# Order and queues of the first loads in an attention and two-MLP kernel

## Chip, cores and metric

The kernel runs on one core of a Trainium2 chip. The metric is the device time of one execution in microseconds; several runs are taken and their median counts.

## What is computed

Causal attention with a bias from running sums, for 4 batches of 8 heads, 576 positions and 64 channels, then two MLPs over the 2304 tokens of 512 channels (2048 inside): the first gated by a clipped linear function, the second by x times its sigmoid.

```python
def _attn_ref(q, k, v, s):
    scores = scale * np.matmul(q, k.transpose(0, 1, 3, 2))
    cum = np.cumsum(np.maximum(s, 0.0), axis=-1)
    bias = -(cum[:, :, :, None] - cum[:, :, None, :])
    scores = np.where(causal, -1000000000.0, scores + np.minimum(bias, 0.0))
    attn = softmax(scores)
    return np.matmul(attn, v)

def _moe_ref(x, w_in, w_out):
    h = x @ w_in
    return (h * np.clip(h + 3.0, 0.0, 6.0) / 6.0) @ w_out

def _moe2_ref(x, w_in, w_out):
    h = x @ w_in
    return (h / (1.0 + np.exp(-h))) @ w_out
```

The weights come in as 64-bit floats. A raw chunk of them (128 x 512 numbers, 512 KB) is turned into 32-bit floats on the chip and split into a high and a low part for the matmuls.

## The kernel before

**Stages.** The queries of a batch are cut into a part A (positions 0 to 255) and a part B (256 to 511, with the last 64 as a tail). A `Head` is one head of one batch and part, and there are 64 of them; the eight of part A of batch 0 come first. The plan runs in slots: nine slots with a head alone, then slots with a head and a step of the first MLP (`first` and `second`, lines 245 to 301). In a slot the current head's scores, mask, maximum and exps are made, the head before it is transposed and multiplied by its v (`av`), and the one before that is put in its place.

**Heads.** `Head.load` (line 394) issues q, k and, for the first 14 heads, v into one tile with a place of its own (lines 413, 414 and 403, 64 KB each). `load_cum` (line 416) puts two rows of running sums below q and k (line 423), which the score matmul (line 512) reads together with them. The first four heads take these rows from the tile `pairs` on the chip, later ones from its copy in memory, `pair_d` (stored at line 875). `pairs` is made from s: load (341), clip and scale (342), scan into `crow` (345), and two copies of it, one on VectorE (349) and one on ScalarE (350). In slot k the head k + 2 is loaded.

**Raw chunks.** `Feed.tick` (line 199) moves the chunks through a pipeline: `load` (147), `fields` on ScalarE and POOL (159 to 161), `join` on VectorE (172 and 176), and two ticks later `high` on ScalarE (120) and `low` on VectorE (187). Three ticks are made before the first slot, then 0.4 in a slot for nine slots, then two. The MLP steps of block 0 use two chunks each.

**Queues and order.** All of these transfers are issued by SP. The program gives the instructions in an order that serves as a priority; a scheduler places them on the engines, and an instruction whose inputs its own model takes to be ready can pass an earlier one. Each engine then runs its list in order. `keep_clock` (line 83) issues matmuls on constants; 34 of them stand at the start, and slots without an MLP step have three each.

Of the kernel before, what the change touches and what calls it, by code (L numbers as in the profile page):

```python
# [11 lines left out]
I32 = mybir.dt.int32  # L12
# [10 lines left out]
def f32(ap):  # L23
    return ap.bitcast(F32)
# [3 lines left out]
def kernel(  # L28
# [15 lines left out]
    nc = tc.nc  # L44
# [10 lines left out]
    T1 = 256  # L55
# [23 lines left out]
    busy = gpool.tile([P, 1024], BF16, tag="gl", name="busy")  # L79
# [3 lines left out]
    def keep_clock(n, beside):  # L83
        for _ in range(n):
            o = idle[:, : beside.shape[-1]]
            nc.tensor.matmul(o, busy[:, :P], beside, start=True, stop=True)
# [1 line left out]
    def heads_of(x):  # L88
        return x.bitcast(BF16).rearrange("p (n two) -> p n two", two=2)[:, :, 1]

    keep_clock(34, busy[:, :512])

    NZ = (NFULL - 1) * P
    cmask = cpool.tile([P, NZ + P], F32, tag="cmask", name="cmask")
# [18 lines left out]
    def pool_copy(o, i):  # L113
        nc.gpsimd.tensor_scalar(  # L114
            out=o, in0=i, scalar1=1.0, scalar2=1.0, op0=ALU.mult, op1=ALU.mult
        )
# [13 lines left out]
    class Chunk:  # L130
        def __init__(self, kind, m, f):
            self.key = (kind, m, f)
            self.src = ((w1i, w1o), (w2i, w2o))[m][kind == "o"][f]
            self.nm = f"{kind}{m}_{f}"
            self.home = wpool, f"{kind}{f}"
# [2 lines left out]
            pool, tag = self.home  # L138
            return pool.tile(shape, dt, tag=tag, name=f"{name}{self.nm}")

        def load(self):
            if self.src.dtype == F32:
                self.val = self.place([P, DM], F32, "raw")
                nc.sync.dma_start(self.val, self.src)
            else:
                raw = self.place([P, 2 * DM], I32, "raw")
                nc.sync.dma_start(raw, self.src.bitcast(I32))
                words = raw.rearrange("p (n two) -> p n two", two=2)
                self.words = words[:, :, 0], words[:, :, 1]

# [38 lines left out]
    class Feed:  # L189


        def __init__(self, keys, hi_eng, lo_eng):
            self.ch = [Chunk(*k) for k in keys]
            self.hi_eng, self.lo_eng = hi_eng, lo_eng
            self.t = 0

        def done(self):
            return self.t >= len(self.ch) + 3 + 2

        def tick(self):  # L200
            n = len(self.ch)
            t = self.t - 3
            lo = self.lo_eng[t % len(self.lo_eng)] if 0 <= t - 2 < n else ""
            if lo:
                self.ch[t - 2].high(self.hi_eng[t % len(self.hi_eng)])
            if 0 <= t < n:
                self.ch[t].fields()
            if lo == "p":
                self.ch[t - 2].low(lo)
            if 0 <= t - 1 < n:  # L210
                self.ch[t - 1].join()
            if lo == "v":
                self.ch[t - 2].low(lo)
            if self.t < n:
                self.ch[self.t].load()
            self.t += 1


# [112 lines left out]
    def bank(kind, shape, name):  # L331
# [6 lines left out]
    srow, crow = [  # L338
        wpool.tile([BH, S], F32, tag=f"{kd}{NF // 2 - 1}", name=f"{kd}row") for kd in "io"
    ]  # L340
# [5 lines left out]
    pairs = wpool.tile([BH, 2, 2 * T1], F32, tag=f"o{NF // 2 - 2}", name="pairs")  # L346
    nc.gpsimd.memset(pairs[:, 0, :T1], 1.0)
    nc.gpsimd.memset(pairs[:, 1, T1:], -1.0)
    nc.vector.tensor_copy(pairs[:, 0, T1:], crow[:, :T1])
    nc.scalar.copy(pairs[:, 1, :T1], crow[:, :T1])  # L350

    def split_rows():

# [16 lines left out]
    class Head:  # L370
# [20 lines left out]
                    (c, 0, w // 2, False), (c, w // 2, w, True)]  # L391
            self.full = [c for c in self.chunks if c < NFULL]

        def load(self):
            b, h, nm, nk, nq = self.b, self.h, self.nm, self.nk, self.nq
            if self.at < 14:

                t = wpool.tile([P, 2 * DM], F32, tag=spare[self.at], name=f"in{nm}")
                self.q2, self.k2 = t[:, :nq], t[:, nq : nq + nk]
                self.qk = t[:, : nq + nk]  # L400
                self.va = t[:, DM + nk :][:, : self.nkc * D].rearrange("p (c d) -> p c d", d=D)
                self.load_qk()
                nc.sync.dma_start(self.va, v1[b, h, :, : self.nkc, :])
                return
            tags = ("qs", "kl") if self.whole and self.slot else ("q2", "k2")
            self.q2 = apool.tile([P, nq], F32, tag=tags[0], name=f"q2{nm}")
            self.k2 = apool.tile([P, nk], F32, tag=tags[1], name=f"k2{nm}")
            self.load_qk()

        def load_qk(self):  # L410
            b, h, nk = self.b, self.h, self.nk
            for r in (slice(0, D), slice(D, 2 * D))[: 1 if self.whole else 2]:
                nc.sync.dma_start(self.q2[r, :], qT[b, h, :, self.q0 : nk])
                nc.sync.dma_start(self.k2[r, :], kT[b, h, :, :nk])

        def load_cum(self):

# [356 lines left out]
    heads = []  # L774
# [3 lines left out]
    feed = Feed([(kd, 0, f) for f in range(NF) for kd in "io"], "a", "v")  # L778
# [3 lines left out]
    def ticks(n):  # L782
        for _ in range(n):
            if not feed.done():
                feed.tick()
# [79 lines left out]
    def at(i):  # L865
        return heads[i] if 0 <= i < len(heads) else None


    loaded = 2
    for hd in heads[:loaded]:  # L870
        hd.load()
    ticks(3)
    for hd in heads[:loaded]:
        hd.load_cum()
    nc.sync.dma_start(pair_d, pairs)
    heads[0].places()
    k = 0
    p1 = p2 = None
    plan = [(True, False)] * (H + 1) + [(i < 55, True) for i in range(68)]
    nslot = 0  # L880
    for has_head, has_step in plan:
        cur = at(k) if has_head else None
        nx = at(k + 1) if has_head else None
        loads = []
        while has_head and loaded < len(heads) and loaded <= k + (
            2
        ):
            loads.append(heads[loaded])
            loaded += 1
        k += has_head and cur is not None  # L890
        tk = [0, 0, 0, 0]
        if not feed.done():
            rate = ((0.4,)*9+(2,))[min(nslot, len(((0.4,)*9+(2,))) - 1)]
            for i in range(4):
                feed_at += rate / 4
                tk[i] = int(feed_at)
                feed_at -= tk[i]
        slot(cur, p1, p2, nx, loads, has_step, tk)
        if nslot == 9:
            split_rows()  # L900
        p1, p2 = cur, p1
        nslot += 1
        if nslot == H + 1:
            p2.av_sum()
            p2 = None
            split1(0)
            turns["s"] = turns["s"][:1]
        if has_step and step in first_step[1:NB1]:
            blk = first_step.index(step)
            assert k - (cur is not None) >= (blk + 1) * H  # L910
            if p2:
                p2.av_sum()
                p2 = None
            if blk == NB1 - 1:
                cx.close()
                xpool = cx.enter_context(
                    tc.tile_pool(name="xlast", bufs=1, side="right", reuse_waits="tile")
                )
            split1(blk)
            if blk == NB1 - 1:  # L920
                break
# [70 lines left out]
    feed = Feed([("o", 1, f) for f in range(NF)], "a", "v")  # L992
# [293 lines left out]
```

## Time and profile before

| | us |
|---|---|
| median of 3 runs | 999.63 |
| lowest and highest | 997.51 and 1001.86 |
| the profiled execution | 1000.54 |
| span of the profiled execution | 998.8 |
| TensorE busy (matmuls) | 970.8 |
| VectorE busy | 737.9 |
| ScalarE busy | 511.0 |
| POOL busy | 317.2 |

The profile is of one execution. PE is TensorE's matmuls, PEld its weight loads, DVE VectorE, ACT ScalarE, POOL GpSimd; SPq and ACTq are the queues on which SP and ScalarE issue DMAs. Times in the trace count from the start of the span. A wait is put down to the releaser that came last by the profile; where a transfer is named that the instruction does not read, it was another one beside it.

### The profile page before, as it was taken

To read this page: it belongs to the slowest core of one execution; us is meant where nothing else is said; L and a number is where in the kernel's file an instruction comes from. 1 tells how busy PE (TensorE), PEld (TensorE's weight loads), DVE (VectorE), ACT (ScalarE), POOL (GpSimd) and SP (SyncE) were. 2 spreads that over 40 slices of the span, in tenths; PEclk is the share of its full clock that TensorE was granted. 3 is DMA by queue.
4 is the path that set the end of the run, shared out by engine and by line. 5 is a ranking of instruction groups with operands and counts; after the bars stand their busy time and mean duration, and the time that the engine had idled before them with its cause. 6 is when DMAs were issued, how large, how long until landed. Compare 5 with 4: busy or idle time off the path is not lost.

```text
span 998.8 us, 17929 instructions
## 1 busy us (share of the span) xinstructions
PE 970.8 (97%) x6268; PEld 891.6 (89%) x6268; DVE 737.9 (74%) x1757; ACT 511.0 (51%) x1177; POOL 317.2 (32%) x323
## 2 busy tenths in 40 slices
PE   8899989999999999999999999999999999999997
PEld 5789979999999999999997877899988989889996
DVE  6899998888789888988866799887574434743343
ACT  6898554555455555555446656564443323432332
POOL 4457853443333443434425566532000000000000
PEclk9999999999999999999999999999999999999999
DMA  5796112312222223222215957434354233442421
GB/s 174 225 302 198 47 40 67 92 46 63 83 77 75 71 59 92 60 64 80 60 39 186 392 212 237 163 116 190 133 195 169 77 145 110 167 154 76 148 74 64
DMA packets 54419, 125.41 MB, mean 126 GB/s; under 512 B 12332, under 2 KB 34076, under 8 KB 51000
## 3 DMA queue, kind: packets, MB, share of 16 engines
q1 hardware_dynamic: 53880, 123.60, 37.3%
q8 instruction: 50, 0.82, 0.3%
q10 hardware_dynamic: 448, 0.66, 0.2%
q14 instruction: 41, 0.34, 0.1%
HBM read 99.52 MB, written 24.69 MB: 124 GB/s over the span
## 4 chain that ended last, share of the span: by engine, by line
PE 70%; DVE 11%; DMA 8%; issue 4%; POOL 4%; SPq 3%; ACT 1%; POOLq 0%; DVEq 0%; ACTq 0%
PE a L1083 6%; PE a L1084 6%; PE a L1085 6%; PE h L1066 5%; PE h L1068 5%; PE h L1067 5%; PE ph L260 4%; PE ph L261 4%; PE ph L262 4%; PE acc L299 4%; PE acc L300 4%; PE acc L301 4%; PE poB L672 4%; DMA rawi<-in_w1i_dram 3%; POOL rawo L161 2%
## 5 line engine op out<-in xcount | busy, mean ns | idle before, releaser
L260 PE MATMUL ph<-xh,wi 128*128 128x256 f32 (+1 forms) x512 | 154.1, 303 | 3.2 <-DVE g L273 3.1
L300 PE MATMUL acc<-gl,wo 128*128 128x256 f32 (+1 forms) x512 | 151.1, 297 | 2.4 <-DVE gl L280 2.4
L261 PE MATMUL ph<-xl,wi 128*128 128x256 f32 (+1 forms) x512 | 151.6, 296 | 0.0
L262 PE MATMUL ph<-xh,wi 128*128 128x256 f32 (+1 forms) x512 | 151.3, 296 | 0.0
L301 PE MATMUL acc<-gh,wo 128*128 128x256 f32 (+1 forms) x512 | 149.8, 294 | 0.0
L1125 ACT ACTIVATE gh<-h 128x384 fp32r<-128x384 f32 x96 | 50.3, 524 | 185.4 <-DVE h L1133 185.3
L299 PE MATMUL acc<-gh,wo 128*128 128x256 f32 (+1 forms) x512 | 143.8, 297 | 0.0
L1083 PE MATMUL a<-wo,gh 128*128 128x512 f32 x288 | 113.5, 394 | 1.4 <-ACT gh L1125 0.9
L1084 PE MATMUL a<-wo,gh 128*128 128x512 f32 x288 | 113.1, 393 | 0.0
L260 PEld LDWEIGHTS ph<-xh,wi 128*128 128x128 f32 x512 | 97.4, 190 | 8.9 <-DVE g L273 2.5
L300 PEld LDWEIGHTS acc<-gl,wo 128*128 128x128 f32 x512 | 96.4, 188 | 6.4 <-DVE gl L280 3.5
L262 PEld LDWEIGHTS ph<-xh,wi 128*128 128x128 f32 x512 | 97.6, 191 | 3.0
L261 PEld LDWEIGHTS ph<-xl,wi 128*128 128x128 f32 x512 | 97.5, 190 | 3.2
L301 PEld LDWEIGHTS acc<-gh,wo 128*128 128x128 f32 x512 | 96.5, 189 | 3.3
L299 PEld LDWEIGHTS acc<-gh,wo 128*128 128x128 f32 x512 | 95.6, 189 | 3.4
L161 POOL TENSOR_SCALAR rawi<-rawi 128x512 int32<-128x512 f32 x32 | 70.0, 2188 | 74.1 <-ACT magi L160 48.4
L1085 PE MATMUL a<-wo,gl 128*128 128x512 f32 x288 | 90.0, 392 | 0.0
L161 POOL TENSOR_SCALAR rawo<-rawo 128x512 int32<-128x512 f32 x32 | 74.5, 2329 | 48.0 <-ACT mago L160 46.3
L1127 DVE TENSOR_TENSOR gl<-h,gh 128x384 fp32r<-128x384 f32 x96 | 53.8, 560 | 39.9 <-ACT h L1126 38.2
L114 POOL TENSOR_SCALAR gh<-g 128x512 fp32r<-128x512 f32 x68 | 50.6, 745 | 92.6 <-DVE g L273 77.4
L1133 DVE TENSOR_TENSOR h<-h,u 128x384 f32<-128x384 f32 x72 | 40.1, 557 | 53.5 <-PE h L1068 53.2
L1066 PE MATMUL h<-x0t,w 128*128 128x384 f32 x192 | 64.9, 338 | 0.7 <-DVE u L1133 0.7
(220 smaller groups left out, 2554.6 us busy)
## 6 DMA issues: line engine op xcount, KB each, us to landing
w<-w_d SPq DMA_DIRECT2D x18, 1792.0 KB
w_d<-w SPq DMA_DIRECT2D x8, 1792.0 KB
k2B<-in_kT_dram SPq DMA_DIRECT2D x64, 144.0 KB
rawi<-in_w1i_dram SPq DMA_DIRECT2D x16, 512.0 KB
rawo<-in_w1o_dram SPq DMA_DIRECT2D x16, 512.0 KB
rawi<-in_w2i_dram SPq DMA_DIRECT2D x16, 512.0 KB
rawo<-in_w2o_dram SPq DMA_DIRECT2D x16, 512.0 KB
q2B<-in_qT_dram SPq DMA_DIRECT2D x64, 80.0 KB
```

Source lines behind the costliest of these rows:

```text
L161: nc.gpsimd.tensor_scalar(out=high, in0=f32(high), scalar1=0.0, scalar2=float(SIGN), op0=ALU.is_lt, op1=ALU.mult,)
L260: nc.tensor.matmul(o, wih[:, cs], xh[c], start=c == 0, stop=False)
L261: nc.tensor.matmul(o, wih[:, cs], xl[c], start=False, stop=False)
L262: nc.tensor.matmul(o, wil[:, cs], xh[c], start=False, stop=c == NDC - 1)
L299: nc.tensor.matmul(a, woh[:, cs], gh[:, jj, :], start=b0, stop=False)
L300: nc.tensor.matmul(a, woh[:, cs], gl[:, jj, :], start=False, stop=False)
L301: nc.tensor.matmul(a, wol[:, cs], gh[:, jj, :], start=False, stop=b1)
L1066: nc.tensor.matmul(ps, w[:, 0, cs], xh[:, c, :], start=c == 0, stop=False)
L1083: nc.tensor.matmul(accs[t], gh[:, k, cs], woh, start=b0, stop=False)
L1084: nc.tensor.matmul(accs[t], gh[:, k, cs], wol, start=False, stop=False)
L1085: nc.tensor.matmul(accs[t], gl[:, k, cs], woh, start=False, stop=b1)
L1127: nc.vector.tensor_tensor(out=gl[:, i, o], in0=g, in1=f32(gh[:, i, o]), op=ALU.subtract)
```

## The change

It loads four heads before the first slot instead of two. Heads 0 and 2 go out on SP's queue, heads 1 and 3 and the first raw chunk on ScalarE's. The two copies that fill `pairs` now stand behind these issues in the program. Then come the four heads' running sums and the store of `pairs`, on SP. The second and third raw chunks follow on SP; ahead of each, POOL copies four numbers of `pairs` into the raw tile's first words, which the chunk's transfer overwrites, so that it has to wait for `pairs`. In the slots a head is loaded three ahead instead of two until 14 are loaded. The first warm-up has 26 matmuls instead of 34. The last hunk, the rate of ticks, is the same numbers written otherwise.

```diff
-    keep_clock(34, busy[:, :512])
+    keep_clock(26, busy[:, :512])
...
-        def load(self):
+        def load(self, queue=nc.sync, behind=None):
...
-                nc.sync.dma_start(raw, self.src.bitcast(I32))
+                if behind is not None:
+                    pool_copy(f32(raw[:1, :4]).rearrange("p (a b) -> p a b", b=2), behind)
+                queue.dma_start(raw, self.src.bitcast(I32))
...
+            self.queue, self.behind = nc.sync, None
...
-                self.ch[self.t].load()
+                self.ch[self.t].load(self.queue, self.behind)
...
-    nc.vector.tensor_copy(pairs[:, 0, T1:], crow[:, :T1])
-    nc.scalar.copy(pairs[:, 1, :T1], crow[:, :T1])
...
-        def load(self):
+        def load(self, queue=nc.sync):
...
-                self.load_qk()
-                nc.sync.dma_start(self.va, v1[b, h, :, : self.nkc, :])
+                self.load_qk(queue)
+                queue.dma_start(self.va, v1[b, h, :, : self.nkc, :])
...
-                nc.sync.dma_start(self.q2[r, :], qT[b, h, :, self.q0 : nk])
-                nc.sync.dma_start(self.k2[r, :], kT[b, h, :, :nk])
+                queue.dma_start(self.q2[r, :], qT[b, h, :, self.q0 : nk])
+                queue.dma_start(self.k2[r, :], kT[b, h, :, :nk])
...
-    loaded = 2
-    for hd in heads[:loaded]:
-        hd.load()
-    ticks(3)
+    loaded = 4
+    queues = nc.sync, nc.scalar, nc.sync, nc.scalar
+    for hd, queue in zip(heads[:2], queues):
+        hd.load(queue)
+    feed.queue = nc.scalar
+    ticks(1)
+    for hd, queue in zip(heads[2:loaded], queues):
+        hd.load(queue)
+    nc.vector.tensor_copy(pairs[:, 0, T1:], crow[:, :T1])
+    nc.scalar.copy(pairs[:, 1, :T1], crow[:, :T1])
     for hd in heads[:loaded]:
         hd.load_cum()
     nc.sync.dma_start(pair_d, pairs)
+    feed.queue, feed.behind = nc.sync, pairs[:1, :, T1 - 1 : T1 + 1]
+    ticks(2)
+    feed.behind = None
...
-        while has_head and loaded < len(heads) and loaded <= k + (
-            2
-        ):
+        while has_head and loaded < len(heads) and loaded <= k + 2 + (loaded < 14):
...
-            rate = ((0.4,)*9+(2,))[min(nslot, len(((0.4,)*9+(2,))) - 1)]
+            rate = 0.4 if nslot < 9 else 2
```

## Rows read from the trace of the kernel before

**Rows 1.** The page: shares of the chain that ended last, by engine.

```profile
PE 70%; DVE 11%; DMA 8%; issue 4%; POOL 4%; SPq 3%; ACT 1%; POOLq 0%; DVEq 0%; ACTq 0%
```

**Rows 2.** Stretch, length; busy PE, PEld, DVE, ACT, POOL (instructions); clock, DMA share, GB/s.

```profile
20.00:30.00 10.00, 8.01 (x55) 6.09 (x54) 7.78 (x36) 8.53 (x28) 3.99 (x2) 1.00 0.47 137
30.00:40.00 10.00, 8.87 (x66) 7.68 (x65) 8.84 (x32) 8.24 (x25) 3.47 (x2) 1.00 0.84 240
40.00:50.00 10.00, 8.95 (x60) 8.56 (x59) 9.18 (x25) 8.29 (x20) 6.19 (x4) 0.83 0.85 272
...
60.00:80.00 20.00, 18.15 (x141) 16.89 (x142) 19.39 (x63) 19.55 (x52) 12.15 (x7) 1.00 0.90 284
...
100.00:150.00 50.00, 43.45 (x335) 40.57 (x335) 49.59 (x108) 29.05 (x65) 33.59 (x26) 0.97 0.17 44
150.00:200.00 50.00, 49.80 (x410) 49.17 (x411) 42.99 (x121) 25.00 (x65) 19.51 (x27) 1.00 0.27 79
```

**Rows 3.** Timeline, warm-up and first score: start, us, engine, line, operation [idle before].

```profile
1.45 9.63 PE L86 MATMUL idle<-busy 128*128 128x512 bf16 x34 [1.45 <-DVE half L101]
...
5.68 4.89 PEld L86 LDWEIGHTS <-busy 128*128 128x128 bf16 x23 [0.28 <-issue]
...
11.42 0.46 PE L512 MATMUL ps0A<-inA 66*128 66x128 f32 x2 [0.35 <-DMA rawi<-in_w1i_dram]
...
12.03 0.29 DVE L534 CUSTOM_DVE_ANT_0 pb0A<-ps0A,cmask 128x128 f32<-128x128 f32 x1 [5.62 <-PE ps0A L512]
```

**Rows 4.** Timeline, from s to the pairs, on ScalarE and VectorE.

```profile
0.72 1.28 ACT L350 ACT_TABLE_LOAD   x1 [0.72 <-PEq L1267]
...
2.64 0.60 DVE L342 TENSOR_SCALAR irow<-irow 32x576 f32<-32x576 f32 x1 [1.25 <-DMA irow<-in_s_dram]
...
4.65 0.40 ACT L350 COPY pairs<-orow 32x256 f32<-32x256 f32 x1 [2.65 <-DVE orow L345]
4.65 0.74 DVE L349 COPY pairs<-orow 32x256 f32<-32x256 f32 x1
```

**Rows 5.** Timeline of SP's queue: when each transfer is issued, and how long that takes.

```profile
0.73 0.41 SPq L341 DMA_DIRECT2D irow<-in_s_dram  x1
...
4.86 0.43 SPq L147 DMA_DIRECT2D rawi<-in_w1i_dram  x1
...
6.42 1.39 SPq L423 DMA_DIRECT2D inA<-pairs  x2
...
11.61 0.48 SPq L413 DMA_DIRECT2D inA<-in_qT_dram  x1
...
14.10 0.49 SPq L413 DMA_DIRECT2D inA<-in_qT_dram  x1
14.63 0.59 SPq L414 DMA_DIRECT2D inA<-in_kT_dram  x1
...
15.90 0.43 SPq L147 DMA_DIRECT2D rawo<-in_w1o_dram  x1
```

**Rows 6.** The chain that ended last, in order of time: start, us, what.

```profile
5.81 5.79 DMA rawi<-in_w1i_dram
...
77.19 5.25 DMA rawi<-in_w1i_dram
```

**Rows 7.** Timeline, head 7: its sums' issue, its score, VectorE behind it.

```profile
24.68 0.29 SPq L423 DMA_DIRECT2D inA<-pair_d  x1
...
27.34 0.46 PE L512 MATMUL ps0A<-inA 66*128 66x128 f32 x2 [1.45 <-DMA inA<-pair_d]
...
27.84 0.29 DVE L534 CUSTOM_DVE_ANT_0 pb0A<-ps0A,cmask 128x128 f32<-128x128 f32 x1 [1.59 <-PE ps0A L512]
```

**Rows 8.** Timeline, two issues on ScalarE's queue at the kernel's end.

```profile
993.90 1.37 ACTq L1105 DMA_DIRECT2D out_dram<-o  x2
```

**Rows 9.** Timeline, a small and a large POOL operation.

```profile
1.33 0.11 POOL L105 MEMSET sums<- 128x5 f32 x1
...
10.33 2.00 POOL L161 TENSOR_SCALAR rawi<-rawi 128x512 int32<-128x512 f32 x1 [5.08 <-DMA rawo<-in_w1o_dram]
```

More of the change, by code (lines that the diff above doesn't have):

```diff
@@ L139, in place @@
             return pool.tile(shape, dt, tag=tag, name=f"{name}{self.nm}")
-        def load(self):
+        def load(self, queue=nc.sync, behind=None):
             if self.src.dtype == F32:
                 self.val = self.place([P, DM], F32, "raw")
-                nc.sync.dma_start(self.val, self.src)
+                queue.dma_start(self.val, self.src)
             else:
                 raw = self.place([P, 2 * DM], I32, "raw")
-                nc.sync.dma_start(raw, self.src.bitcast(I32))
+                if behind is not None:
+                    pool_copy(f32(raw[:1, :4]).rearrange("p (a b) -> p a b", b=2), behind)
+                queue.dma_start(raw, self.src.bitcast(I32))
                 words = raw.rearrange("p (n two) -> p n two", two=2)
@@ L408, in load, with load_qk @@
             self.load_qk()
-        def load_qk(self):
+        def load_qk(self, queue=nc.sync):
             b, h, nk = self.b, self.h, self.nk
             for r in (slice(0, D), slice(D, 2 * D))[: 1 if self.whole else 2]:
-                nc.sync.dma_start(self.q2[r, :], qT[b, h, :, self.q0 : nk])
-                nc.sync.dma_start(self.k2[r, :], kT[b, h, :, :nk])
+                queue.dma_start(self.q2[r, :], qT[b, h, :, self.q0 : nk])
+                queue.dma_start(self.k2[r, :], kT[b, h, :, :nk])
         def load_cum(self):
```

## The prediction

> **What bounds the kernel now.** I read the page first: TensorE is busy for 970.8 of 998.8 us and holds 70% of the chain of waits, so most of this kernel can't be moved by a change to its first few microseconds [rows 1]. Then the busy times by stretch, to see where another engine sets the pace. The reader should see three stages there [rows 2]. Up to 12 us the engines wait for the first head (below). From there to 150 us VectorE is the fullest engine or close to it: 7.78 of 10 us from 20 to 30, then 8.84 and 9.18 of 10, 19.39 of 20 from 60 to 80, and 49.59 of 50 from 100 to 150. From 150 us on TensorE is (49.80 of 50). The stage in the middle does a fixed amount of VectorE work: masks and maxima of the heads, and the joining of the 32 raw chunks. So a microsecond won ahead of it is kept only if VectorE starts earlier or idles less, and it then reaches the end of the kernel, as TensorE behind 150 us has a fixed amount of work too.
>
> Then the start itself. VectorE's first work on a head begins at 12.03 us after 5.62 us of idle time, and it waits for the first score matmul at 11.42 us [rows 3]. That matmul had an idle TensorE for only 0.35 us: 34 warm-up matmuls hold it from 1.45 us to 11.08 us (9.63 us). The rest of the wait is put down to a raw chunk, but the score doesn't read one. It reads head 0's q, k and the two rows of running sums, whose transfers SP issues at 6.42 us, behind three raw chunks issued from 4.86 to 6.24 us [rows 5]. The last of these lands at 11.60 us (5.81 and 5.79) [rows 6]. So the sums lie in the queue behind 1.5 MB.
>
> Last, SP's own list. From 11.61 to 24.97 us, when head 7's sums are issued, it issues without a pause [rows 5, 7]. A head is four DMAs, q 0.49, k 0.59, v 0.59 and sums 0.29, about 2.1 us with the gaps; a raw chunk is 0.43 [rows 5, 7]. The issue at 11.61 us is the 18th on SP, and it starts as the 10th lands at 11.60 us [rows 5, 6]; so SP seems to run at most eight ahead. One head is visibly late from this: sums issued at 24.68 us, score at 27.34 us after 1.45 us of idle TensorE, VectorE idle for 1.59 us [rows 7].
>
> **The change, part by part.** *Warm-up.* Eight matmuls go. 23 of them take 4.89 us, so 0.213 us each and 1.70 us in all: TensorE is free at 9.38 us, not 11.08 [rows 3]. That is the floor for the first score; from 11.42 us it can win 2.0 us and no more.
>
> *When the sums are ready.* Both copies start at 4.65 us, behind the scan; VectorE's ends at 5.39 us [rows 4]. ScalarE's ends at 5.05 us, but after the change seven issues (head 1, a raw chunk, head 3) stand ahead of it on ScalarE. Two issues on its queue took 1.37 us at the kernel's end [rows 8], SP's 0.43 to 0.59 each; seven of 0.55 from 0.72 us end at 4.6 us. The 1.28 us table load, now hidden in ScalarE's first idle time [rows 4], comes behind the issues in the worse order. That makes 4.6 + 1.28 + 0.40 = 6.3 us. Lower bound 5.4 us (VectorE's copy ends last). Upper bound: if the eight in flight count both queues, head 3's q is the 12th and waits for the 4th, head 0's v, which is issued at about 2.5 us and lands 1.9 us later (as s: issued at 0.73 us, used at 2.64 us [rows 4, 5]); then three issues, load and copy: 4.4 + 1.7 + 1.28 + 0.40 = 7.8 us. I take 6.3, as the load is shown ahead of the first activation and the joint count isn't shown.
>
> *First score.* In before, 5.0 us lie between the issue of the sums and the score, with 1.5 MB ahead. Where little is ahead a head's last rows take 2.7 us (24.68 to 27.34) [rows 7]. Now 0.5 MB is left ahead, on the other queue: a third of the difference on top of 2.7 gives 3.5 us as an estimate, so 6.3 + 3.5 = 9.8 us, with 8.1 us (the warm-up then sets 9.4) and 12.8 us as ends. Gain 1.6 us, between 2.0 and -1.4.
>
> *SP.* It has s and heads 0 and 2 issued at 4.86 us, as now with heads 0 and 1 [rows 5]. From 6.3 us come four sums (0.70 each, from 1.39 for two), the store of the pairs (0.43 with gap) and two raw chunks (0.95): 10.5 us, where head 4 starts. Now head 4 starts at 14.10 us: 3.6 us ahead, between 2.1 and 4.5 by the bounds of the sums. The stop at 11.6 us for the third chunk goes. What is late next: raw chunks stay at their place in the loop, and heads are now loaded three ahead up to the 14th, so one more head (2.1 us) stands before each chunk on SP. The chunk of 15.90 us thus wins 1.5 us, not 3.6 (0 to 2.4); behind the 14th head the 2.1 us come back. The load of head 7, late now, comes 3.6 us earlier by SP's list, and 0.4 more as a chunk now follows it instead of standing ahead [rows 5]. VectorE will reach it 1.6 us earlier by the start, and 1.59 us more are wanted: 4.0 against 3.2, so this idle time goes.
>
> *Two small copies on POOL* (one pair into the first words of a raw tile) make the chunks wait for the sums. The nearest rows are a 0.11 us fill and the 2.00 us sign step [rows 9]; four elements are like the fill. POOL sits idle up to 10.33 us, so they cost nothing. If they came late, the two chunks behind them and then head 4 on SP would wait as long, and SP's lead of 3.6 us covers that.
>
> *Raw chunks two and three* land about 5 us later than now. Their conversion filled ScalarE, POOL and VectorE ahead of and beside the first heads. It is done in the heads' stretch now, but no matmul needs them before the first step at 31 us, so I count nothing; at worst two chunks' ScalarE work, 2.6 us, falls due beside the exps.
>
> *Sum.* By VectorE: 1.6 at the start and 1.6 at head 7 make 3.2 us. By SP and the transfers, which fill 0.85 to 0.90 of the transfer engines from 40 to 80 us [rows 2]: 1.5 us rising to 3.6. I take 3.0: the profiled execution of 1000.54 us (998.8 of span and 1.7 around it) becomes 997.5. Its time is 0.9 above the median of the runs, 999.63, so the forecast is 996.6 us.
>
> The Trainium skill (DMA: Bandwidth & Descriptors, "Issuing engines are not separate DMA queues") says that a second issuing engine saves only the time to start transfers, which is usually small beside the transfer. The trace has it otherwise here: 13 us of SP without a pause while the transfer engines are half used [rows 2, 5]. By the page the sum would keep the start's 1.6 us alone, which lies in the second rival.
>
> **Rivals.** *More than counted.* VectorE idles another 2.0 us in short waits from 30 to 50 us (1.16 and 0.82), and TensorE's granted clock has a mean of 0.83 from 40 to 50 us [rows 2], which is 1.7 us of its ten. With inputs early, both could go: 3.2 + 2.0 is 5.2 us, with the clock 6.9; 992.7 to 994.4. Against it: most of these waits are between VectorE, ScalarE and TensorE, with no transfer in them.
>
> *Absorbed.* The heads come earlier, but the chunks don't, as each stands behind one more head, and the transfers bind from 30 to 82 us; the chain runs through them as late as 77.19 us [rows 6]. Gain 0 to 1.5 us: 998.2 to 999.6. For it: the chain; against it: VectorE is full in the same stretch. A second queue that gives nothing ends in the same place: SP's lead of 3.6 us less seven issues of 0.55 is nil, and at most the start's 1.6 us stay (0.05 of the chance).
>
> *Slower.* ScalarE's issues hold up its copy. It decides from the point at which the copy ends so late that the sums land after 11.42 us: 8.7 us with 2.7 us of landing, 6.4 us with 5.0. At the upper bounds the first score starts at 12.8 us, 1.4 us late, SP's lead of 2.1 us goes to the extra head, and the time is 1001.0. By the scheduler's order a changed start can also move work far behind it; that could cost more, but no row gives it a size.
>
> **How the numbers follow.** Forecast (994.6 to 998.2) 0.50; more than counted 0.20; absorbed 0.18; slower 0.12, half of it by over 5 us through order. 0.5% is 5.0 us, about what can be told from no change here. So faster 0.20, same 0.74, slower 0.06. The range from 993.0 to 1001.2 leaves out some 0.05 at either end.
>
> **What would show it.** Right: first score between 9.4 and 10 us, VectorE's first long idle 1.5 to 2 us shorter, no wait for head 7's rows, head 4's q issued near 10.5 us on SP, raw chunk four near 14.4 us, VectorE's full stretch ending near 147 us. Wrong: ScalarE's copy past 8 us; a score waiting for sums behind the ScalarE queue's chunk; chunk times in the loop as now; or a stretch from 150 us on that is longer than now.

## The result and the profile after

The changed kernel took 1005.08 us (median, 1003.34 to 1007.04) against 999.68 us for the kernel before: ratio 1.0055, interval 1.0038 to 1.0072. Run again on another chip it had 1.0027 (1.0009 to 1.0044). The forecast was 996.6 us with a range to 1001.2, so the change is slower, by 0.3 to 0.6%, where a small gain was expected, and lies outside the range. The profiled execution has 1006.70 us, span 1004.9.

Read the start first: TensorE's and ScalarE's timelines (start, us, engine, line, operation, idle time before and what ended it). The lines of the changed kernel have moved: the score matmul is L513, the AV matmul L688, the first MLP step L263.

```profile
1.44 7.50 PE L86 MATMUL idle<-busy 128*128 128x512 bf16 x26 [1.44 <-DVE half L101]
10.11 0.46 PE L513 MATMUL ps0A<-inA 66*128 66x128 f32 x2 [1.17 <-DMA inA<-pairs]
...
36.20 0.36 PE L263 MATMUL ph<-xh,wi 128*128 128x256 f32 x1
...
5.18 1.28 ACT L879 ACT_TABLE_LOAD   x1 [5.18 <-DMA inA<-in_v_dram]
6.47 0.40 ACT L879 COPY pairs<-orow 32x256 f32<-32x256 f32 x1
```

The warm-up ends at 8.94 us, the sums are ready at 6.87 us behind seven issues and the table load, and the first score starts at 10.11 us instead of 11.42 [rows 3]. So the start is won, by 1.31 us. But the first step of the MLP begins at 36.20 us; before it was 31.14 us. The loss comes between the two. Busy time by stretch, with the columns of [rows 2]:

```profile
12.00:20.00 8.00, 7.40 (x30) 5.65 (x28) 4.97 (x25) 7.17 (x23) 3.32 (x2) 0.50 0.87 271
20.00:30.00 10.00, 10.00 (x47) 8.51 (x47) 7.82 (x28) 5.19 (x16) 2.66 (x2) 0.56 0.50 148
30.00:40.00 10.00, 8.84 (x55) 7.22 (x55) 7.20 (x29) 8.30 (x26) 4.03 (x2) 0.83 0.78 237
```

From 20 to 30 us TensorE is busy for all of 10 us, at a granted clock of 0.56, and does 47 matmuls; before it did 55 in 8.01 us at a clock of 1.00 [rows 2]. ScalarE falls from 8.53 to 5.19 us, as it gets less to do. VectorE is as busy as before and isn't the bound: TensorE is. Summed over windows of 2 us up to 300 us, TensorE's idle time is 16.1 us (before: 16.5), and its busy time times the missing share of the clock is 13.1 us (before: 3.3). That is 9.4 us more lost, less 1.7 us of warm-up that is gone, so 7.7 us against a span that is 6.1 us longer; the sum does not close by 1.6 us. So the time shows as low clock: 1.2 GHz, the lower of its two levels, from 11.8 to 28.8 us and again at 32 to 36, 49 to 53 and 94 to 97 us. The late stretches are as before (150 to 200 us: TensorE 50.00 of 50, before 49.80 [rows 2]), and TensorE's share of the chain that ended last is 71%, before 70% [rows 1].

Is the clock the cause or a sign? The second view is the order in which TensorE works. Head 4's score (the first that reads `pair_d`) and the AV of heads 0 and 1:

```profile
17.16 0.77 PE L513 MATMUL ps0A<-inA 66*128 66x128 f32 x2 [0.60 <-DMA inA<-pair_d]
...
19.22 1.38 PE L688 MATMUL poA<-inA,thA 128*128 128x64 f32 x6
20.39 0.74 PE L513 MATMUL ps0A<-inA 66*128 66x128 f32 x2
...
22.42 1.38 PE L688 MATMUL poA<-inA,thA 128*128 128x64 f32 x6
```

In the kernel before the AV of heads 0 and 1 runs at 16.04 and 18.46 us, and head 4's score behind both at 19.50. Here head 4's score stands ahead of both in TensorE's list and head 5's ahead of the second, and TensorE runs its list in order. SP's timeline shows why head 4 comes only at 17.16 us:

```profile
7.54 0.47 SPq L414 DMA_DIRECT2D inA<-in_qT_dram  x1
8.19 2.58 SPq L424 DMA_DIRECT2D inA<-pairs  x4
...
11.33 0.35 SPq L149 DMA_DIRECT2D rawo<-in_w1o_dram  x1
11.79 0.38 SPq L149 DMA_DIRECT2D rawi<-in_w1i_dram  x1
...
15.62 0.42 SPq L149 DMA_DIRECT2D rawo<-in_w1o_dram  x1
```

So does the chain that ended last (start, us, what):

```profile
2.43 5.09 DMA inA<-in_v_dram
...
13.50 3.57 DMA inA<-pair_d
```

The scheduler put head 4's q ahead of the sums on SP, where it waited for a transfer to land at 7.52 us; the sums went out at 8.19 us; then came two raw chunks, and head 4's own sums behind them, landing at 17.07 us.

### The profile page after: what moved, and what is told of

It reads as the page before. It is cut to its first block, busy times and chain, and to the rows that moved or that the text cites. A ratio compares the mean times of both kernels' runs of the same rounds, so it can differ in the third digit from the quotient of the medians.

```text
span 1004.9 us, 17918 instructions
## 1 busy us (share of the span) xinstructions
PE 977.3 (97%) x6260; PEld 898.1 (89%) x6260; DVE 739.9 (74%) x1757; ACT 510.7 (51%) x1177; POOL 317.0 (32%) x325
## 4 chain that ended last, share of the span: by engine, by line
PE 71%; DVE 13%; POOL 5%; issue 5%; DMA 5%; ACT 1%; SPq 0%; POOLq 0%; DVEq 0%; ACTq 0%
PE a L1091 6%; PE a L1092 6%; PE a L1093 6%; PE h L1074 5%; PE h L1076 5%; PE h L1075 5%; PE ph L263 4%; PE ph L264 4%; PE ph L265 4%; PE acc L302 4%; PE acc L304 4%; PE acc L303 4%; PE poB L673 3%; POOL rawo L163 2%; POOL rawi L163 2%
## 5 line engine op out<-in xcount | busy, mean ns | idle before, releaser
L263 PE MATMUL ph<-xh,wi 128*128 128x256 f32 (+1 forms) x512 | 154.2, 303 | 4.1 <-DVE g L276 2.6
L263 PEld LDWEIGHTS ph<-xh,wi 128*128 128x128 f32 x512 | 97.4, 190 | 10.2 <-DVE g L276 3.9
L114 POOL TENSOR_SCALAR gh<-g 128x512 fp32r<-128x512 f32 x68 | 50.8, 748 | 100.4 <-DVE g L276 88.6
```

The lines of the kernel that those rows point to most:

```text
L263: nc.tensor.matmul(o, wih[:, cs], xh[c], start=c == 0, stop=False)
```

## The experiments

The theories moved as the runs came in, and the expectations keep them as they stood. At first: *the clock* (idle time ahead of the first score lets TensorE's clock fall, and that costs the time) against *the loads* (queue, lookahead, raw chunks). Later: *the order*. The scheduler writes a list for each engine from the program and its own estimates of time, so one warm-up more or less can give another list. To see that, the lists of the compiled programs were compared row by row, without buffer numbers and warm-ups. TensorE's lists start as follows (s4 is head 4's score, A0 head 0's AV):

```
before, 34 or 26 warm-ups       s0 s1 s2 s3 A0 A1 s4 s5 A2 s6 A3
list A: change, 16 to 26        s0 s1 s2 s3 s4 A0 s5 A1 s6 s7 A2
list B: change, 27 to 34        s0 s1 s2 s3 A0 A1 s4 s5 A2 s6 A3
list C: sums first, 16 to 25    s0 s1 s2 s3 A0 s4 A1 s5 s6 A2 s7
list D: sums first, 26 and 30   s0 s1 s2 s3 A0 A1 s4 A2 s5 A3 s6
```

Within a list all 6210 rows of TensorE in the traces are the same (warm-ups and the other matmuls on constants left out), and so are the rows of the other engines. A and B have the same row in some 4980 of TensorE's 6210 places, and they differ on the other engines too: the same row in 1228 of VectorE's 1757 places, 881 of ScalarE's 1186 and 496 of SP's 593. So a list stands for the order on all engines. "Sums first" means that all three raw chunks stand behind the sums on SP. All results, sorted by how many AVs stand ahead of the first score that reads `pair_d`; the clock is the median of the runs' mean granted clocks. List D has two there, as B has, and a third between the scores of heads 4 and 5:

| kernel | list, AVs ahead | median us | ratio to before | interval | clock |
|---|---|---|---|---|---|
| changed | A, 0 | 1005.08 | 1.0055 | 1.0038 to 1.0072 | 0.988 |
| changed, again | A, 0 | 1006.03 | 1.0027 | 1.0009 to 1.0044 | 0.988 |
| changed, 22 full + 32 small | A, 0 | 1005.93 | 1.0042 | 1.0027 to 1.0058 | 0.988 |
| sums first, 16 | C, 1 | 1005.96 | 1.0041 | 1.0018 to 1.0063 | 0.986 |
| sums first, 25 | C, 1 | 1006.54 | 1.0046 | 1.0030 to 1.0062 | 0.987 |
| changed, lookahead two | own, 1 | 1004.09 | 1.0036 | 1.0022 to 1.0050 | 0.980 |
| before, lookahead three | own, 1 | 1006.14 | 1.0054 | 1.0037 to 1.0071 | 0.993 |
| changed, edge | own, 1 | 1004.86 | 1.0030 | 1.0018 to 1.0042 | 0.983 |
| changed, 30, lookahead two | own, 2 | 1006.29 | 1.0049 | 1.0026 to 1.0073 | 0.989 |
| changed, 30, one queue | own, 2 | 1003.25 | 1.0017 | 1.0003 to 1.0030 | 0.995 |
| before, 26 | as before, 2 | 1000.47 | 0.9996 | 0.9973 to 1.0019 | 0.992 |
| changed, 34 | B, 2 | 1000.38 | 1.0008 | 0.9984 to 1.0033 | 0.996 |
| changed, 30 | B, 2 | 999.44 | 0.9989 | 0.9977 to 1.0002 | 0.994 |
| changed, 28 | B, 2 | 1000.68 | 0.9986 | 0.9964 to 1.0007 | 0.994 |
| changed, 27 | B, 2 | 1000.89 | 0.9983 | 0.9967 to 0.9999 | 0.994 |
| sums first, 25, edge | own, 2 | 1001.08 | 0.9989 | 0.9971 to 1.0006 | 0.988 |
| sums first, 30 | D, 2 | 998.09 | 0.9970 | 0.9946 to 0.9994 | 0.993 |
| sums first, 26 | D, 2 | 997.52 | 0.9968 | 0.9945 to 0.9990 | 0.991 |
| sums first, 26, again | D, 2 | 997.03 | 0.9954 | 0.9939 to 0.9970 | 0.992 |

The kernel before had medians from 999.68 to 1002.49 us on the chips of these runs, so kernels of different runs are compared by the ratio.

**The warm-up put back (e1).**

```diff
-    keep_clock(26, busy[:, :512])
+    keep_clock(34, busy[:, :512])
```

> The changed kernel with the old first warm-up of 34 matmuls instead of 26; queues and order of the loads stay changed. Clock theory (TensorE ran dry from 8.94 to 10.11 us, its granted clock fell to 0.50 from about 11.7 to 28.5 us, and 6 us were lost there): warm-up ends near 10.7 us, first score within 0.3 us of it, granted clock 1.00 from 12 to 28 us, time 993 to 999 us. Order theory (the changed queues and the later second and third chunk cost the time, the low clock is beside the point): 1003 to 1007 us whatever the clock does.

1.0008: the loss is gone, and the clock is 1.00 from 12 to 38 us (it falls to 0.50 at 40.6 to 50.8 us). It also has list B, which was seen only later.

**The short warm-up alone (e2).**

```diff
-    keep_clock(34, busy[:, :512])
+    keep_clock(26, busy[:, :512])
```
(in the kernel before)

> The kernel before with 26 warm-up matmuls instead of 34 and nothing else of the change. Its sums still land at about 11.3 us, so TensorE stands idle from 8.94 to 11.4 us. Clock theory: granted clock near 0.50 for a long part of 12 to 30 us, 1003 to 1009 us. Order theory: the idle time costs nothing, as the score can't start earlier anyway: 998 to 1001 us, clock 1.00.

0.9996. TensorE's timeline:

```profile
1.45 7.38 PE L86 MATMUL idle<-busy 128*128 128x512 bf16 x26 [1.45 <-DVE half L101]
11.36 0.60 PE L512 MATMUL ps0A<-inA 66*128 66x128 f32 x2 [2.53 <-DMA inA<-pairs]
```

and the stretches:

```profile
12.00:20.00 8.00, 8.00 (x32) 6.78 (x32) 6.58 (x27) 4.48 (x16) 4.04 (x2) 0.50 0.49 147
20.00:30.00 10.00, 9.39 (x64) 7.71 (x62) 8.81 (x39) 9.45 (x30) 3.00 (x2) 0.91 0.55 139
```

TensorE idles for 2.53 us and then runs at 0.50 up to about 21.8 us, with the list of the kernel before, and no time is lost at the end: the scores of heads 4 to 6 are 2.3 to 2.7 us late, but head 7's is 0.8 us late, where the stall of [rows 7] takes it up. So a fall of the clock in these heads isn't by itself the loss.

**Warm-up of 30 (e3), lookahead two (e4).**

```diff
-    keep_clock(26, busy[:, :512])
+    keep_clock(30, busy[:, :512])
```

> The changed kernel with 30 warm-up matmuls, which end near 9.8 us, 0.3 us ahead of the first score at 10.11 us. Clock theory: no long idle time, clock stays at 1.00 up to 28 us, 993 to 999 us, and up to 0.9 us under the kernel with 34. Order theory: 1003 to 1007 us, as with 26.

```diff
-        while has_head and loaded < len(heads) and loaded <= k + 2 + (loaded < 14):
+        while has_head and loaded < len(heads) and loaded <= k + 2:
```
(e4, with 26 warm-ups)

> The changed kernel (26 warm-up matmuls) with heads loaded two ahead in the slots, as before, not three. Clock theory: first score still at about 10 us after more than 1 us of idle TensorE, clock still low from 12 to 28 us, 1003 to 1007 us. Order theory, with the extra head ahead of each raw chunk as its cause: chunks are issued about 2 us earlier, 998 to 1002 us.

e3 has 0.9989. It is the change as it was meant: clock 1.00 up to 40 us, the scores from head 3 on 0.9 to 3.8 us ahead (head 7's at 23.50 us, before 27.34 [rows 7]), head 7's idle time gone. And the lead is lost again, by stretch:

```profile
20.00:30.00 10.00, 8.73 (x65) 7.04 (x65) 9.81 (x38) 9.12 (x29) 5.41 (x3) 1.00 0.47 135
30.00:40.00 10.00, 7.10 (x48) 5.68 (x48) 8.23 (x32) 8.23 (x26) 4.11 (x2) 1.00 0.78 242
40.00:50.00 10.00, 8.87 (x53) 8.53 (x52) 8.04 (x21) 7.76 (x17) 6.80 (x5) 0.66 0.94 312
```

and on SP:

```profile
29.00 0.43 SPq L149 DMA_DIRECT2D rawo<-in_w1o_dram  x1
...
34.55 0.43 SPq L149 DMA_DIRECT2D rawo<-in_w1o_dram  x1
```

The raw chunks go out at 29.00 and 34.55 us; before it was 28.91 and 34.54. TensorE is busy for 7.10 us of the ten from 30 on (before 8.87 [rows 2]), and its clock then falls to 0.66. e4 (1.0036) loses as the changed kernel does, so the loss doesn't need the lookahead.

**All raw chunks behind the sums (e5), and two mixtures (e6, e8).**

```diff
-    feed.queue = nc.scalar
-    ticks(1)
...
-    ticks(2)
+    ticks(3)
```

> The changed kernel with 26 warm-up matmuls and the first raw chunk, too, behind the running sums (on SP), so that 0.5 MB less is under way while the sums are made. Clock theory (the idle time of TensorE ahead of and just behind the first score lets its clock fall): if the first score comes by 9.3 us, the clock stays at 1.00 from 12 to 28 us with only 26 matmuls, and the time is 998 to 1001 us; if a gap of 0.5 us or more is left, the clock falls again and it is 1003 to 1008 us. Count theory (fewer warm-up matmuls as such lower the clock, whatever the gap): clock low from 12 us on and 1003 us or more in any case.

0.9968 with 26 warm-ups, and the clock holds at 1.00 from 8 to 32 us. The count of warm-ups isn't by itself what decides.

e6 joins 30 warm-ups with lookahead two; e8 has 30 warm-ups and issues all on SP:

```diff
-    queues = nc.sync, nc.scalar, nc.sync, nc.scalar
+    queues = nc.sync, nc.sync, nc.sync, nc.sync
...
-    feed.queue = nc.scalar
```

> The changed kernel with 30 warm-up matmuls (clock held) and heads loaded two ahead, so that each raw chunk has one head less before it on SP. If the place of the chunks is what eats the lead of the heads (2 to 3 us at the eighth head, nothing at the end with 30 matmuls): chunks two to six are issued 1 to 2 us earlier than with three ahead, and the time is 995 to 998 us. If the lead is lost to idle TensorE between the ninth head and the first MLP steps whatever the chunks do: 998 to 1002 us.

> The changed kernel with 30 warm-up matmuls and all loads on SP, none on ScalarE's queue. If the second queue is worth its seven issues (my step): the sums are issued near 9.5 us, the first score comes near 12 us after 2 us of idle TensorE, the clock falls as with 26 and the time is 1003 to 1008 us. If the second queue gives nothing: first score by 10.3 us and 998 to 1001 us.

e6 has 1.0049 and its clock falls at 27 to 50 us; e8 has 1.0017 and no fall up to 80 us. In e8 the first of the sums goes out at 9.03 us and the first score comes at 10.97, not near 12 as expected; in e3 it is 8.10 and 10.67, right behind the warm-up. By the ratios e8 takes 2.8 us more than e3 (0.28%), but the lists differ too (on TensorE 5282 of 6210 places agree), so how much of that is the queue's isn't shown. The Trainium skill (DMA: Bandwidth & Descriptors, "Issuing engines are not separate DMA queues") says that a second issuing engine saves only the time to start the transfers and calls that usually small. The trace agrees at the start: 0.93 us earlier for the sums, where head 0's v alone takes 5.09 us to land in the changed kernel.

**Three ahead alone (e7),** in the kernel before:

```diff
-        while has_head and loaded < len(heads) and loaded <= k + (
-            2
-        ):
+        while has_head and loaded < len(heads) and loaded <= k + 2 + (loaded < 14):
```

> The kernel before with only the three-ahead loading of heads (up to the 14th). My prediction priced the late seventh head at 1.6 us: if that step holds alone, the wait at 25.9 to 27.3 us goes and the time is 997.5 to 999.5 us. If a head issued earlier only pushes chunks and sums behind it on SP: 999.5 to 1003 us.

1.0054. It was to take away head 7's stall, and it costs 5 us, again with a score ahead of the second AV.

**Sums first with 26 again, 16 and 30 (e9 to e11), the change with 28 (e12).** e9 is e5's program; in the others one number differs:

```diff
-    keep_clock(26, busy[:, :512])
+    keep_clock(16, busy[:, :512])
```
(e10; 30 in e11, and 28 in e12 without e5's edit)

> The same program as in the run with 26 warm-ups and all three raw chunks behind the sums, here as the reference for the two below on one chip. It had 997.52 us (995.49 to 1002.17), ratio 0.9968 to the kernel before. Expected by every theory: 996 to 999 us, first score right behind the warm-up, granted clock 1.00 from 8 to 32 us.

> The same order of loads, with 16 warm-ups: ten times 0.213 us less, so TensorE is free at 7.9 us, and as the rows of sums land at about 9 to 9.5 us it stands idle for 1.0 to 1.6 us ahead of the first score, about as in the changed kernel (1.17 us). The first score comes up to 0.7 us earlier than with 26. Theory of the gap (idle time ahead of the first score makes the granted clock fall, and it costs what the heads then need): clock at or near 0.50 for 10 us or more between 11 and 30 us, heads 4 to 6 us late behind it, 1001 to 1006 us. Rival (the place of the raw chunks and the order around them made the changed kernel slow, the clock is only beside it): 996 to 999 us, whatever the clock shows, and the 0.7 us from the start may be added.

> The same order of loads, with 30 warm-ups: TensorE free at 10.8 us, no idle time ahead of the first score, which comes 0.8 us later than with 26. Theory of the gap: clock 1.00 as with 26, and the 0.8 us is all that is lost at the start: 997 to 999.5 us. Rival (a larger count of warm-ups helps by itself): below 996.5 us. Order rival: anything from 995 to 1003, with the heads at their old times up to 30 us and the difference behind that.

> The changed kernel with 28 warm-ups, between 26 (1005.08 us, clock 0.50 from 12 to 28 us) and 30 (999.44 us, clock 1.00 there). TensorE is free at 9.37 us, the score at about 10.1 to 10.4, so the idle time ahead of it is 0.7 to 1.0 us. Theory of the gap: the result goes with the clock of the profiled run; if it falls in 10 to 30 us the time is 1003 to 1006, if it holds 999 to 1000.5. Rival (order, clock beside it): the time doesn't go with the clock, for example a fall and 999 to 1000, or no fall and 1004.

0.9954, 1.0041 and 0.9970: that looked like the idle time ahead of the score. But in e10 the clock did not fall behind that idle time. TensorE:

```profile
8.22 0.46 PE L513 MATMUL ps0A<-inA 66*128 66x128 f32 x2 [1.53 <-DMA inA<-pairs]
...
16.86 0.46 PE L513 MATMUL ps0A<-inA 66*128 66x128 f32 x2 [2.42 <-DVE sums L561]
```

and the stretches:

```profile
12.00:18.00 6.00, 3.24 (x24) 2.41 (x22) 2.08 (x14) 5.78 (x15) 3.23 (x2) 1.00 1.03 339
18.00:30.00 12.00, 11.67 (x51) 10.10 (x51) 9.14 (x33) 7.96 (x23) 5.78 (x4) 0.52 0.55 143
```

It is 1.00 up to 18 us and falls behind a second hole, ahead of head 4's score. And e12 speaks against the theory: clock near 0.50 from 12 to 18 us, and 0.9986. Here the lists were compared.

**One warm-up more (e13), list C without the idle time (e14), list A with a longer warm-up (e15), the changed kernel again (e16).**

```diff
-    keep_clock(26, busy[:, :512])
+    keep_clock(27, busy[:, :512])
```
(e13; in e14 25, on top of e5's edit; e15:)

```diff
-    keep_clock(26, busy[:, :512])
+    keep_clock(22, busy[:, :512])
+    keep_clock(32, busy[:, :64])
```

> The changed kernel with 27 warm-ups, one more than it has: 0.21 us less of the idle time ahead of the first score. Compared row by row, the compiled kernels fall into two orders of work: with up to 26 warm-ups TensorE's list is the same as in the changed kernel, with 27 to 34 it is another one, the same for 27, 28, 30 and 34, and parts from it at the seventh instruction behind the warm-up. Theory of the clock (the idle time makes the granted clock fall, and that costs the 5 us): the idle time is still 1 us, so clock 0.50 for 5 us or more and 1003 to 1006 us. Theory of the order (the list that the scheduler writes for 26 costs the 5 us, whatever the clock does): 999.5 to 1001.5 us, as with 28 and 30, even where the clock falls.

> All three raw chunks behind the sums, 25 warm-ups instead of 26. With 25 and fewer the list is that of the run with 16 warm-ups (1005.96 us), with 26 and 30 that of the fast ones (997.03 and 998.09). 25 warm-ups end at about 9.4 to 9.9 us and the sums land before that, so there is no idle time ahead of the first score, as with 26. Theory of the idle time ahead of the first score: 996.5 to 999 us, as with 26. Theory of the order: 1003 to 1007 us, as with 16.

> The changed kernel with 22 full warm-ups and 32 of 64 columns in place of the last 4. For the scheduler they take the same time: the order of the work is the one of the changed kernel, instruction by instruction. On the chip each small one needs its own load of weights, so the warm-up should end 0.8 to 1.7 us later, at 9.8 to 10.6 us, and close the idle time ahead of the first score. Theory of the clock: 1.00 from 12 to 28 us, and 999 to 1001 us. Theory of the order: 1003.5 to 1006 us, though the clock holds there.

> The changed kernel itself, here as the reference of the three above on one chip: 1003 to 1006 us by every theory, the clock near 0.50 from 12 to 28 us.

e13: 0.9983, where A has 1.0027 to 1.0055. TensorE:

```profile
11.13 0.46 PE L513 MATMUL ps0A<-inA 66*128 66x128 f32 x2 [1.64 <-DMA inA<-pairs]
...
17.69 1.38 PE L688 MATMUL poA<-inA,thA 128*128 128x64 f32 x6
19.50 0.85 PE L688 MATMUL poA<-inA,thA 128*128 128x64 f32 x6
20.18 0.44 PE L513 MATMUL ps0A<-inA 66*128 66x128 f32 x2
...
31.16 0.40 PE L263 MATMUL ph<-xh,wi 128*128 128x256 f32 x1
```

and one stretch:

```profile
12.00:20.00 8.00, 8.00 (x39) 6.64 (x37) 5.10 (x26) 6.31 (x22) 0.63 (x2) 0.57 0.79 254
```

There is more idle time ahead of the score (1.64 us) than the changed kernel has (1.17 us), the score is later and the clock at 0.57 from 12 to 20 us, and yet the first MLP step starts at 31.16 us. e14 is the reverse: no idle time ahead of the score, the clock 1.00 there, and 1.0046.

```profile
9.58 0.39 PE L513 MATMUL ps0A<-inA 66*128 66x128 f32 x2
...
14.84 0.88 PE L688 MATMUL poA<-inA,thA 128*128 128x64 f32 x6 [0.25 <-ACT thA L120]
16.93 0.48 PE L513 MATMUL ps0A<-inA 66*128 66x128 f32 x2 [1.21 <-DMA inA<-pair_d]
18.71 1.38 PE L688 MATMUL poA<-inA,thA 128*128 128x64 f32 x6
```

The same stretch of e9, with one warm-up more and list D:

```profile
9.56 0.39 PE L513 MATMUL ps0A<-inA 66*128 66x128 f32 x2
...
13.81 0.78 PE L688 MATMUL poA<-inA,thA 128*128 128x64 f32 x6
15.02 0.85 PE L688 MATMUL poA<-inA,thA 128*128 128x64 f32 x6
17.59 0.39 PE L513 MATMUL ps0A<-inA 66*128 66x128 f32 x2
```

In both head 4's score starts around 17 us; in e14 it waits there for its rows. In e9 TensorE has done two AVs by then, in e14 one, and the other comes at 18.71 us. But the wait for the rows isn't what kept it back: an AV reads `thA`, ScalarE's copy of the transposes. ScalarE in e14:

```profile
14.69 0.66 ACT L161 ACTIVATE rawi<-rawi 128x512 int32<-128x512 uint32 x1
...
16.90 0.45 ACT L120 COPY thA<-pt0A 128x384 f32<-128x384 f32 x1
```

and in e9:

```profile
13.90 0.46 ACT L120 COPY thA<-pt0A 128x384 f32<-128x384 f32 x1
...
14.76 0.66 ACT L161 ACTIVATE rawi<-rawi 128x512 int32<-128x512 uint32 x1
```

In e14 head 1's transposes end at 13.65 us, but ScalarE converts two raw chunks first, and the copy ends at 17.35 us, behind the start of head 4's score; in e9 the copy comes first. The changed kernel is alike: head 0's copy ends at 17.40 us, behind a chunk's conversion (14.94 to 16.16 us), and head 4's score had its rows by then. In e10, of the same list as e14, it is otherwise: the copy ends at 16.09 us, and head 4's score, which starts at 16.86, does keep the AV back. ScalarE's order is thus a rival to the place of the score, and no run tests it.

e15 missed its aim: the 32 small matmuls were over at 9.10 us, and 1.29 us of idle time and the fall remained; it stands as one more run of list A. e16 answers part of e15's question by chance: in its profile the idle time ahead of the score is 0.59 us and the clock falls only about 17 us, not 12, and its span is 1004.4 us. TensorE, and the stretches:

```profile
10.52 0.46 PE L513 MATMUL ps0A<-inA 66*128 66x128 f32 x2 [0.59 <-DMA inA<-pairs]
```

```profile
12.00:18.00 6.00, 3.21 (x23) 2.71 (x22) 3.97 (x21) 5.18 (x17) 1.32 (x1) 0.93 0.85 263
18.00:30.00 12.00, 12.00 (x58) 9.86 (x56) 8.60 (x34) 7.83 (x22) 4.64 (x3) 0.61 0.61 171
```

The same list with five microseconds less of low clock ahead of head 4's score gives the same time, and that score comes at 17.52 us, in the changed kernel's first profile at 17.16.

**The place in the list (e17, e18).** An edge for the scheduler puts head 4's score behind the AV of head 1:

```diff
+    def behind_av(at):
+        return tc.issue_after(heads[at - 3].last.ins) if at in (4,) else ExitStack()
...
-                nc.tensor.matmul(
-                    pS[:n, :], self.q2[:d, qs], self.k2[:d, a:z], start=True, stop=True
-                )
+                with behind_av(self.at):
+                    nc.tensor.matmul(
+                        pS[:n, :], self.q2[:d, qs], self.k2[:d, a:z], start=True, stop=True
+                    )
...
-                    nc.tensor.matmul(
+                    self.last = nc.tensor.matmul(
```
(the last hunk in `av_whole`)

> The changed kernel with 26 warm-ups and one more edge for the scheduler: head 4's score matmuls come behind head 1's AV matmuls on TensorE. In the changed kernel's list head 4's score stands ahead of the AV of heads 0 and 1, and waits there for head 4's rows (17.16 us), so AV starts at 19.22 and the first MLP step at 36.20 us, while with 27 warm-ups AV of heads 0 and 1 stands ahead of it, starts at 17.69, and the step at 31.16 us. Theory of this place: first AV by 17.5 us or earlier, first MLP step at 29 to 32 us, 999 to 1002 us. Rival (another place of the list, or the clock of this stretch): AV earlier, but the first MLP step at 34 us or later, 1003 to 1006 us.

> The same edge in the kernel with all three raw chunks behind the sums and 25 warm-ups (1006.54 us; with 26 warm-ups and the AV of heads 0, 1 and 2 ahead of head 4's score it had 997.03 and 997.52). In the slow list head 4's score stands between the AV of heads 0 and 1. Theory of this place: 997 to 1000 us, first MLP step at 28.5 to 30 us, no idle time of 2 us on TensorE from 13 to 18 us that AV of head 1 could fill. Rival: the edge gives back less than 2 of the 9 us, 1004.5 us or more.

TensorE in e18:

```profile
14.83 0.88 PE L689 MATMUL poA<-inA,thA 128*128 128x64 f32 x6 [0.25 <-ACT thA L120]
18.48 1.38 PE L689 MATMUL poA<-inA,thA 128*128 128x64 f32 x6
19.65 0.74 PE L514 MATMUL ps0A<-inA 66*128 66x128 f32 x2
...
35.25 0.36 PE L263 MATMUL ph<-xh,wi 128*128 128x256 f32 x1
```

e18: 0.9989 against 1.0046, so by the ratios two thirds of the way from list C to list D (0.9954 to 0.9970) came back with one edge. The edge also moves other rows (5135 of TensorE's 6210 places are as in e14), and head 1's AV comes at 18.48 us, in e14 at 18.71, so the gain isn't that AV's. It isn't all: list D has an AV between the scores of heads 4, 5 and 6; in e18 the three scores follow each other. And the way is not as expected: the first MLP step starts at 35.25 us, later than in e14 (31.38), so its start isn't the measure of the loss. e17 gained nothing beyond the spread of the runs of list A (1.0030): the scheduler put head 5's score in the place that head 4's had to leave, and it waits there longer. TensorE in e17:

```profile
17.72 0.88 PE L689 MATMUL poA<-inA,thA 128*128 128x64 f32 x6 [0.24 <-ACT thA L120]
21.27 0.76 PE L514 MATMUL ps0A<-inA 66*128 66x128 f32 x2 [2.67 <-DMA inA<-pair_d]
```

So e17 doesn't test the place.

**What follows.** Shown: kernels with one list agree (A 1.0027 to 1.0055, B 0.9983 to 1.0008, C 1.0041 and 1.0046, D 0.9954 to 0.9970, before 0.9996 to 1), whatever the clock does ahead of the first score and behind it, and one warm-up that changes the list moves the time by 0.4 to 0.9%. Not shown: which rows of a list cost the time. The kernels with fewer than two AVs ahead of head 4's score all have 1.0027 or more, but e6 has two and 1.0049, e8 two and 1.0017, e18 recovers two thirds, and the lists differ in many rows on every engine; ScalarE's order is an untested rival. Open, too, is how much of the loss goes through the clock. In the profiles' first 300 us TensorE stands at the lower level for 20 to 27 us in lists A and C, 7 to 14 in list B and the kernel before, 10 to 21 in list D; but e18 has 24 us with 0.9989, and e8 has 10 us with 1.0017. Over the runs of the changed kernel and of all the others, each set against its own mean, 0.01 less of mean clock goes with 4.3 us more (157 runs, correlation -0.61). By that slope, as an estimate, list A's clock of 0.988 against list B's 0.994 would be 2.6 us of some 5 us between them.

## Why the prediction was wrong

- *Warm-up and first score.* Right in time: TensorE free at 8.94 us (said 9.38), sums ready at 6.87 (6.3, at most 7.8), first score 10.11 (9.8), gain 1.31 (1.6). The table load did come behind the issues.
- *The failed step.* The eight warm-ups were booked as 1.70 us of TensorE and a floor for the first score. They also decide which list the scheduler writes: with 27 the same change has 0.9983, with 26 it has 1.0027 to 1.0055. The text named this ("by the scheduler's order a changed start can also move work far behind it") without a size and with half of 0.12 as its chance. The named mechanism of that rival, sums landing after 11.42 us, did not happen. Nor had the sum a term for the clock, which the changed kernel's profile shows at its lower level from 11.8 to 28.8 us.
- *The pace.* VectorE was read as the fullest engine from 12 to 150 us. It fits list B (VectorE 9.81 of 10 us from 20 to 30 in e3). In list A TensorE is full at 0.56 of its clock; a reading of busy shares doesn't carry over to another order.
- *SP.* Head 4 was to start at 10.5 us and the fourth chunk at 14.4. Head 4's q went at 7.54, ahead of the sums, its own sums at 13.50, and the chunk at 15.62: 0.28 us won, not 1.5. That the eight in flight count both queues was held as an upper bound. The joint count is what happened, but it stopped head 4's q on SP, not head 3's: ScalarE's seven issues end at 5.15 us.
- *Two later chunks* were counted at nothing. No run isolates them. They stand ahead of head 4's sums, which took 3.57 us to land, but with all three there the best times came too (list D). The ScalarE work beside the exps that was held as the worst case does appear: 14.94 to 16.16 us in the changed kernel, ahead of an exp and of head 0's copy.
- *Head 7.* In list B its idle time goes, as said (e3: 3.8 us ahead). In the changed kernel its score is at 27.32 us, as before. Three ahead alone doesn't do it (e7). SP's issues "without a pause" were misread, too: in the kernel before, head 7's q itself held SP for 2.01 us, where others took 0.47 to 0.49, and most of head 7's 1.45 us of idle time can come from that:

```profile
21.34 2.01 SPq L413 DMA_DIRECT2D inA<-in_qT_dram  x1
```

- *POOL's copies.* Right: 0.19 us each, at 7.04 and 7.20 us.
- *The sum.* Without the accident of the list (27 to 34 warm-ups) the change has 0.9983 to 1.0008, so between 1.7 us of gain and 0.8 of loss where 3.0 of gain were forecast. That is the rival *Absorbed*: in e3 the chunks go out as before, and the lead of the heads ends at the first MLP steps. Its chance of 0.18 was too low, since the prediction's own figure for the chunk's gain, 1.5 us, was half of the sum.

The version with the sums first and 26 warm-ups beats both kernels: 0.9954 (0.9939 to 0.9970) and 0.9968 (0.9945 to 0.9990).

## What to carry to other kernels

Where a scheduler writes the order, compare the lists of the two compiled kernels first: an edit that looks like a cost of 1.7 us can change hundreds of rows, and on every engine. Look there for work that stands ahead of what another engine waits for, as ScalarE's conversions stand ahead of the copy in e14; which such row cost the time wasn't found here. Keep pairs with the same list as controls, and vary a number by one until the list flips, to tell the edit from the list. A low clock in the profile asks what made the engine wait before it; it isn't yet the reason of the loss.

## What the hardware showed that was not expected

- TensorE's clock fell to 0.50 behind 1.17 us (changed kernel), 1.64 us (e13) and 2.53 us (e2) of idle time, but not behind 1.53 us in e10, where it held until a second hole of 2.42 us. No rule is drawn from these.
- SP's eighth transfer waited from 4.83 to 7.54 us for one that it had issued at 2.43 us, with only seven of its own before it and seven of ScalarE's beside. In the order of both queues together the two are eight apart, as the 18th and the 10th were before. This is the compiled program's limit: it gives its transfers eight semaphores in turn, over both queues, and a transfer waits for the last one with its own (the trace has the same semaphore for these two). What the chip itself would allow isn't shown.
- Head 0's v, 64 KB, took 5.09 us to land; a raw chunk of 512 KB was issued on the other queue 0.28 us after it. That the chunk is the reason isn't shown.
- The same 26 warm-up matmuls took 7.38 us (e2), 7.50 (changed kernel) and 8.48 (e16). They start 0.427 us apart and go over to 0.216, at 5 us in the changed kernel and at 7 us in e16. The view gives a granted clock of 1.00 for both parts, but the traces' clock records begin only at 4.95 and 6.94 us, so for the slower part the clock wasn't recorded; half the pace is what the lower of the two levels would give. So the end of a warm-up is no fixed point, and the 0.213 us per matmul of the prediction holds only for its later part.
